# Batch 0's loads dealt anew among three DMA queues, four casts moved to ScalarE, and a block's first sums queued two groups sooner

## The chip, the cores and the metric

One core of one Trainium2 chip. The metric is the device time of one execution in microseconds, median of several executions. A core has five engines: TensorE (PE), VectorE (DVE), ScalarE (ACT), GpSimd (POOL) and SyncE (SP), each of which has its own list of instructions. In the traces here what stands behind a waiting instruction waits too: in the kernel before, VectorE's squares stand 6.60 us behind a transpose whose input has not landed. DMAs are issued from SyncE's, ScalarE's or GpSimd's queue, in that engine's order.

## The reference

Eight batches of 3008 rows. Attention without softmax, gated by u, then a two-layer network:

```python
scores = (z @ z.T) / S                        # z: 3008 x 64
attn   = np.maximum(scores, 0.0) ** 2
x      = u * (attn @ v)                       # u, v: 3008 x 256
h      = x @ w_in                             # 256 -> 2048
g      = h * (1 / (1 + np.exp(-1.702 * h)))
out    = g @ w_out                            # 2048 -> 256
```

## The kernel before

TensorE makes scores (`sc`) in blocks of 256 by 512; ScalarE applies the ReLU (`rl`), VectorE squares (`a`). The scores are symmetric, so half of the blocks are not computed twice: SyncE turns a square block `a` into `tt` by a DMA transpose. The six chunks of 512 rows then gather attention times V in `o`, VectorE multiplies by the turned u (`ut`) into `xt`, and the network follows. The second matmul of the network uses seven products in place of eight, which needs sums of blocks of `g` (S1 to S4, tile `s`), made by VectorE.

The start of batch 0, cut to the parts that change:

```python
def first_cast(g):                            # z to f16, twice, for the first transposes
    m = g % CB * CB
    for c in range(2):
        dve.tensor_copy(ZT["st"][g // CB][:, m:m + CB, c, :], ZT["f"][g // CB][:, m:m + CB, :])

def load_v(b, n0):                            # 4 blocks of V
    ...
    by_pool = b == 0 and n0 < 3 * VB
    dst, eng = V16[b][:, n0:n0 + VB], pool    # GpSimd's DMA casts f32 to f16 on the way
    if by_pool:                               # or: plain f32 load, and GpSimd itself casts
        dst, eng = pa.tile([P, VB, D], F32, ...), act if n0 < 2 * VB else sp
    ...

def load_u(b, i):                             # chunk i of u: 4 DMAs of 128 KB
    uq = pu.tile([P, CH // QW, QW, NCC], F32, name="uq", tag="uq")
    ...
        pool.dma_start(uq[...], src[:, :, cs])

def turn_unit(b, i, jp, a):                   # the transposes, all in SyncE's queue
    ...
    sp.dma_start_transpose(TT[b, i, cj][...], a...)
```

A chunk's steps are numbered, and tables say at which step a load or a turn of u is programmed: an entry `(i, n): k` means chunk i, step n, item k. Loads are programmed on GpSimd; the table `LOADW` holds the loads of W1 and W2. In chunks 2 and 3 of batch 0, step 23 holds a marker on GpSimd that waits for TensorE; what GpSimd has programmed behind it waits too:

```python
def post(last):
    sig = pool.nop()
    for m in last:
        tc.add_manual_dep(sig.ins, m.ins.name, SYNC, reason="row tiles of one bank")
    return sig
...
TURN0 = {(i, (38, 28)[i] if i < 2 else NJ + 4 if i < NCH - 1 else 12): i for i in range(NCH)}
LOAD0 = {(1, 14): 2, (2, 12): 3, (2, NJ + 20): 4, (4, 8): 5}                  # loads of u
LOADW = {(3, 12): 0, (3, 20): 1, (3, 28): 2, (3, 36): 3, (4, 16): 4, ...}     # loads of W1, W2
```

Of the kernel before, what the change touches and what calls it, by code (L numbers as in the profile page):

```python
# [15 lines left out]
def kernel(  # L16
# [13 lines left out]
    AF = mybir.ActivationFunctionType  # L30
# [6 lines left out]
    NJ = (S + P - 1) // P  # L37
# [4 lines left out]
    CB = CH // P  # L42
# [4 lines left out]
    NFG = NFF // FFG  # L47
    QW = 32
# [7 lines left out]
    dve, act, pe, sp, pool = nc.vector, nc.scalar, nc.tensor, nc.sync, nc.gpsimd  # L56
# [21 lines left out]
    ZT, V16, UQ, UT, XT, unit, TT = {}, {}, {}, {}, {}, {}, {}  # L78
# [37 lines left out]
            for h in range(2):  # L116
                eng.dma_start(zf[h * SREM:(h + 1) * SREM, m1 + CB - 1, :], z[0, S0:S])

    def first_cast(g):
        m = g % CB * CB  # L120
        for c in range(2):
            dve.tensor_copy(ZT["st"][g // CB][:, m:m + CB, c, :], ZT["f"][g // CB][:, m:m + CB, :])

    def first_zt(g):

# [33 lines left out]
    VB = 4  # L159
# [3 lines left out]
    def load_v(b, n0):  # L163

        if n0 == 0:
            V16[b] = pz.tile([P, NJ, D], F16, name="V16", tag="V16")
        by_pool = b == 0 and n0 < 3 * VB
        dst, eng = V16[b][:, n0:n0 + VB], pool
        if by_pool:
            dst, eng = pa.tile([P, VB, D], F32, name="vst", tag="tt", bufs=14), act if n0 < 2 * VB else sp  # L170
        full = min(VB, NJ - 1 - n0)
        eng.dma_start(dst[:, :full, :], v[b, n0 * P:(n0 + full) * P].rearrange("(n p) c -> p n c", p=P))
        if full < VB:
            for h in range(2):
                eng.dma_start(dst[h * SREM:(h + 1) * SREM, full, :], v[b, S0:S])
        if by_pool:
            for n in range(0, VB, 2):
                pool.tensor_copy(V16[b][:, n0 + n:n0 + n + 2], dst[:, n:n + 2])

    def width(i):  # L180
        return CH if i < NCH - 1 else LAST

    def load_u(b, i):
        n = width(i)
        uq = pu.tile([P, CH // QW, QW, NCC], F32, name="uq", tag="uq")
        src = u[b, i * CH:i * CH + n].rearrange("(q t) c -> t q c", t=QW)
        for k in range(P // QW):
            cs = slice(k * NCC * QW, (k + 1) * NCC * QW)
            pool.dma_start(uq[k * QW:(k + 1) * QW, :n // QW].rearrange("t q c k -> t q (c k)"), src[:, :, cs])  # L189
        UQ[b, i] = uq  # L190

    def turn_u(b, i):
# [96 lines left out]
    def full(b):  # L289

        return NCH - 2 if b < B - 1 else NCH - 1
# [65 lines left out]
    def blocks(b):  # L357

        return [(i, CH if i < NCH - 1 or b % 2 else LFULL) for i in range(NCH)]

    def up_group(b, q):
        k, fg = divmod(q, NFG)
        i, n = blocks(b)[k]
        hg = ps2.tile([P, FFG, CH], F32, name="hg", tag="ps2")
        for e in range(FFG):
            ff = fg * FFG + e
            for c in range(NCC):
                pe.matmul(  # L368
                    hg[:, e, :n], W1[:, c, ff * P:(ff + 1) * P], XT[b, i][:, c, :n],
                    start=(c == 0), stop=(c == NCC - 1),  # L370
                )
        if fg % 2 == 0:
            GT[b, k, fg // 2] = pa.tile([P, CB, CH], F16, name="gt", tag="tt", bufs=14)
        g = GT[b, k, fg // 2][:, (fg % 2) * FFG:(fg % 2 + 1) * FFG, :n]
        gf = pw.tile([P, FFG, CH], F32, name="gf", tag="gf")
        act.activation(gf[:, :, :n], hg[:, :, :n], AF.Gelu_apprx_sigmoid, scale=1.0 / FSC)  # L376
        if q >= LAGY and q % 4 == 1:
            act.activation(g, gf[:, :, :n], AF.Copy, scale=FSC)  # L378
        else:
            dve.tensor_scalar(g, gf[:, :, :n], FSC, None, ALU.mult)  # L380
        for s_ in [SUMS.pop(0) for _ in range(min(len(SUMS), 1 + (len(SUMS) > 8)))]:
            s_()
        if k < nst(b) and fg == NFG - 1:
            SUMS.extend(left_sums(b, k))



# [4 lines left out]
    def nst(b):  # L392
        return NCH - 1 + b % 2

    SUMS, ST = [], {}
# [26 lines left out]
        g = GT[b, k, h].rearrange("p f (m o t) -> p f m o t", o=2, t=P)  # L422
        return g[:, :, :, odd, :]

    def left_sums(b, k):
        out_ = []
        for name in ("S1", "S2", "S3", "S4"):
            for h in range(2):
                out_.append(lambda name=name, h=h: left_sum(b, k, name, h))
        return out_  # L430

    def left_sum(b, k, name, h):
        a11, a12, a21, a22 = left(b, k, h, 0), left(b, k, h + 2, 0), left(b, k, h, 1), left(b, k, h + 2, 1)
        if name == "S3":
            ST[b, k, name, h] = a21
            dve.tensor_tensor(a21, a11, a21, ALU.subtract)
            return
        s_ = ST[b, k, name, h] = pa.tile([P, CB, 2, P], F16, name="s", tag="a", bufs=26)
        if name == "S1":
            dve.tensor_tensor(s_, a21, a22, ALU.add)  # L440
        elif name == "S2":
            dve.tensor_tensor(s_, ST[b, k, "S1", h], a11, ALU.subtract)  # L442
        else:
            dve.tensor_tensor(s_, a12, ST[b, k, "S2", h], ALU.subtract)  # L444
# [117 lines left out]
    TURN0 = {(i, (38, 28)[i] if i < 2 else NJ + 4 if i < NCH - 1 else 12): i for i in range(NCH)}  # L562
    LOAD0 = {(1, 14): 2, (2, 12): 3, (2, NJ + 20): 4, (4, 8): 5}
    TURN = {(1, NJ + 4): 2, (2, NJ + 4): 3, (4, NJ + 4): 4, (5, 8): 5}
    LOADW = {(3, 12): 0, (3, 20): 1, (3, 28): 2, (3, 36): 3, (4, 16): 4, (4, 22): 5, (4, 28): 6, (4, 34): 7}
    LOAD = {(3, NJ + 20): 4, (4, NJ + 5): 5}

    FIRST_ZT, FIRST_CAST = {16: 4, 25: 5}, {7: 4, 17: 5}
# [23 lines left out]
        load_v(0, n0)  # L592
    first_z(2 * CB, 4 * CB, sp)
    first_z(4 * CB, NJ, sp)
    load_v(0, 3 * VB)
    load_v(0, 2 * VB)
    for n0 in (4 * VB, 5 * VB):
        load_v(0, n0)
    warm_up(7)
    for g in range(2):  # L600
# [9 lines left out]
        post_()  # L610
    turns[0]()
    take(0, 1)
    for i in range(2):
        load_u(0, i)

    for b in range(B):
        nup = NCH * NFG
        more = b + 1 < B
        sched = SCHED0 if b == 0 else SCHED if more else SCHED_LAST
        turn, load = (TURN, LOAD) if b else (TURN0, LOAD0)  # L620
        head = 0
        for i in range(NCH):
            host = b + 1 if more and i == NCH - 1 else b
            if host > b:
                fill(host)
                LATE.append(host)
            for n, step in enumerate(attend(b, i, b == 0 and i < 2)):
                if b == 0 and i == 0 and n == 3:
                    turns[1]()
                if b == 0 and i == 0 and n in FIRST_CAST:  # L630
                    first_cast(FIRST_CAST[n])
                if b == 0 and i == 0 and n in FIRST_ZT:
                    first_zt(FIRST_ZT[n])()
                if (i, n) in turn:
                    turn_u(b, turn[i, n])
                if (i, n) in load:
                    load_u(b, load[i, n])
                if b == 0 and (i, n) in LOADW:
                    load_w(LOADW[i, n])
                if more and (i, n) == (NCH - 2, 2):  # L640
                    load_z(b + 1)
                if (b, i, n) == (0, NCH - 1, NJ + 4):
                    for sum_ in weight_sums():
                        sum_()
                take(host, sched[i].get(n, 0))
                if i == full(b) and n >= HEAD and (n - HEAD) * LAGY // (2 * NJ - 10) >= head and head < LAGY:
                    up_group(b, head)
                    head += 1
                step()
        late.sort(key=lambda t: t[0])  # L650
        if more:
            for i in range(2):
                load_u(b + 1, i)
            for n0 in range(0, NJ, VB):
                load_v(b + 1, n0)
        prods = products(nst(b))
        for q in range(head, nup):
            if more and q in (head + 14, head + 20):
                k = int(q == head + 20)
                turn_u(b + 1, k)  # L660
                load_u(b + 1, k + 2)
            up_group(b, q)
            product(b, *prods.pop(0))
            if q >= 30 and q % 2 and late:
                late.pop(0)[1]()
        steps = [lambda kp=kp: product(b, *kp) for kp in prods]
        if nst(b) < NCH:
            k = NCH - 1
            steps += [lambda s=s: down(b, k, s) for s in range(blocks(b)[k][1] // P)]
        for step in steps:  # L670
            step()
            for sum_ in [SUMS.pop(0) for _ in range(min(len(SUMS), 1 + (len(SUMS) > 4)))]:
                sum_()
            for _, turn_it in [late.pop(0) for _ in range(min(len(late), 1 + (len(steps) < 10)))]:
                turn_it()
        LATE.clear()
        if more:
            while late:
                late.pop(0)[1]()
            take(b + 1, 2)  # L680
# [30 lines left out]
```

## Time and profile before

| | kernel before |
|---|---|
| time, median of 3 executions | 1209.84 us (1204.06 to 1211.1) |
| span of the profiled execution | 1206.6 us |
| TensorE busy / idle | 1187.5 / 19.1 us |
| wait at u of chunk 0 (hole 1) | 4.46 us at 31.09 |
| wait at the 10th transpose (hole 2) | 4.78 us at 51.65 |
| granted clock in 30 to 40 and 50 to 60 us | 0.83 |
| waits for the sums `s`, start to start | 0.67 + 0.37 us, after four of the eight batches |

How to read it: a hole is a stretch in which TensorE, the busiest engine, stands idle. The lines behind the table stand in the prediction below. In them a timeline line reads: start, duration, engine, source line, operation, output and inputs, how many instructions are merged, and in brackets the idle time before and who ended it. The prediction explains the columns of a window line; numbers in parentheses there count instructions.

### The profile page before, as it was taken

How to read it: one execution, taken by the hardware profiler on the slowest of the kernel's cores; microseconds unless marked ns; L12 is line 12 of the kernel's file. 1: busy time of each engine (PE TensorE's matmuls, PEld its weight loads, DVE VectorE, ACT ScalarE, POOL GpSimd, SP SyncE). 2: the span in 40 equal slices, each digit the busy share in tenths (PEclk: the TensorE clock that was granted, in tenths of full speed). 3: DMA queues.
4: the chain of work that ended last, by engine and by line, in shares of the span. 5: the costliest groups of instructions: out<-in, count | busy, mean ns of one | idle time of the engine just before them, and what ended most of it. 6: DMA issues, size and time to landing. Idle time of an engine off the chain costs nothing.

```text
span 1206.6 us, 27543 instructions
## 1 busy us (share of the span) xinstructions
PE 1187.5 (98%) x11427; PEld 722.9 (60%) x11427; DVE 819.4 (68%) x1319; ACT 828.9 (69%) x983; POOL 228.4 (19%) x328
## 2 busy tenths in 40 slices
PE   7899999999999999999999999999999999999998
PEld 2245775457754677546765467654775547855576
DVE  5579756577666785577775777557776477664776
ACT  6587866678666786568865688647876478672785
POOL 4144010331003310023101231013300142001000
PEclk9899999999999999999999999999999999999999
DMA  9999469765698657876567767794578955695012
GB/s 162 158 132 133 97 146 169 92 97 118 118 165 94 94 133 135 135 87 110 132 132 141 77 106 149 145 129 76 94 149 145 125 85 104 146 159 98 1 36 71
DMA packets 371102, 141.02 MB, mean 117 GB/s; under 512 B 313376, under 2 KB 364320, under 8 KB 370976
## 3 DMA queue, kind: packets, MB, share of 16 engines
q1 hardware_dynamic: 310528, 94.67, 43.8%
q0 software_dynamic: 59088, 43.34, 24.3%
q8 instruction: 89, 1.46, 0.5%
q10 hardware_dynamic: 1360, 1.25, 0.3%
q14 instruction: 37, 0.30, 0.1%
HBM read 60.29 MB, written 24.64 MB: 70 GB/s over the span
## 4 chain that ended last, share of the span: by engine, by line
PE 92%; DVE 3%; DMA 2%; ACT 2%; issue 1%; POOL 1%; ACTq 0%; DVEq 0%
PE o L327 38%; PE hg L368 26%; PE st L469 20%; PE sc L227 6%; PE yp L525 2%; ACT gf L376 1%; DMA uq<-in_u_dram 1%; DMA vst<-in_v_dram 1%; DMA tt<-a 1%; DVE gt L380 0%; DVE s L444 0%; DVE s L442 0%; DVE s L440 0%; ACT rl L241 0%; DVE y L485 0%
## 5 line engine op out<-in xcount | busy, mean ns | idle before, releaser
L376 ACT ACTIVATE gf<-hg 128x1024 f32<-128x1024 f32 (+1 forms) x384 | 385.6, 1004 | 137.5 <-PE hg L368 114.6
L241 ACT ACTIVATE rl<-sc 128x1024 f16<-128x1024 f32 x309 | 303.4, 1027 | 163.6 <-PE sc L227 155.7
L327 PEld LDWEIGHTS <-V 64*128 64x128 f16 (+1 forms) x4052 | 239.9, 95 | 242.4 <-issue 15.7
L368 PE MATMUL hg<-xt,W 128*128 128x512 f16 (+1 forms) x1408 | 354.6, 374 | 0.0
L380 DVE TENSOR_SCALAR gt<-gf 128x1024 f16<-128x1024 f32 (+1 forms) x320 | 223.0, 697 | 144.9 <-ACT gf L376 141.5
L327 PE MATMUL o<-a,V 64*128 64x512 f16 (+3 forms) x2286 | 305.3, 370 | 0.2 <-DVE a L255 0.2
L255 DVE TENSOR_TENSOR a<-rl 128x1024 f16<-128x1024 f16 x274 | 189.0, 695 | 163.0 <-ACT rl L241 162.9
L189 POOL DMA_DIRECT2D uq<-in_u_dram x192 | 129.7, 683 | 627.5 <-PE sc L227 372.5
L327 PE MATMUL o<-tt,V 64*128 64x512 f16 (+1 forms) x1510 | 234.9, 377 | 4.8 <-DMA tt<-a 4.8
L368 PEld LDWEIGHTS <-W 128*128 128x128 f16 x1536 | 139.3, 98 | 119.3 <-issue 2.6
L469 PEld LDWEIGHTS <-gt 128*128 128x128 f16 x2816 | 169.5, 98 | 31.9
L469 PEld LDWEIGHTS <-s 128*128 128x128 f16 x2112 | 127.8, 98 | 29.6 <-DVE s L442 4.2
L227 PE MATMUL sc<-ZT 64*128 64x512 f16 (+1 forms) x688 | 122.1, 368 | 5.5 <-ACT rl L241 4.5
L469 PE MATMUL st<-WT,s 128*128 128x128 f16 x1408 | 93.1, 219 | 2.9 <-DVE s L442 2.8
L469 PE MATMUL st<-WT,gt 128*128 128x128 f16 x1408 | 93.0, 219 | 0.0
L469 PE MATMUL st<-W,gt 128*128 128x128 f16 x1408 | 92.3, 219 | 0.0
L479 ACT ACTIVATE uP<-st 128x256 f32<-128x256 f32 x132 | 49.7, 376 | 27.7 <-PE st L469 15.5
L227 PEld LDWEIGHTS <-ZT 64*128 64x128 f16 x688 | 39.0, 94 | 49.3 <-issue 14.4
L485 DVE SCALAR_TENSOR_TENSOR y<-st,uP 128x256 f32<-128x256 f32 x132 | 54.5, 418 | 20.4 <-ACT uP L479 11.4
L378 ACT ACTIVATE gt<-gf 128x1024 f16<-128x1024 f32 (+1 forms) x64 | 66.0, 1031 | 2.0
L344 DVE TENSOR_TENSOR xt<-o,ut 128x512 f16<-128x512 f32 x80 | 51.3, 683 | 22.7 <-PE o L327 22.7
L196 DVE STREAM_TRANSPOSE ut<-uq 128x1024 f32<-128x1024 f32 (+1 forms) x48 | 58.2, 1213 | 6.6 <-DMA uq<-in_u_dram 6.6
(50 smaller groups left out, 613.3 us busy)
## 6 DMA issues: line engine op xcount, KB each, us to landing
uq<-in_u_dram POOLq DMA_DIRECT2D x160, 128.0 KB, 3.6
out_dram<-y SPq DMA_DIRECT2D x40, 512.0 KB, 3.5
V<-in_v_dram POOLq DMA_DIRECT2D x37, 256.0 KB, 6.3
tt<-a SPq DMA_TRANSPOSE x232, 3.7
uq<-in_u_dram POOLq DMA_DIRECT2D x32, 112.0 KB, 4.9
V<-in_v_dram POOLq DMA_DIRECT2D x8, 192.0 KB, 8.0
out_dram<-y POOLq DMA_DIRECT2D x4, 384.0 KB, 3.2
zst<-in_z_dram POOLq DMA_DIRECT2D x7, 192.0 KB, 8.5
```

The lines of the kernel that those rows point to most:

```text
L189: pool.dma_start(uq[k * QW:(k + 1) * QW, :n // QW].rearrange("t q c k -> t q (c k)"), src[:, :, cs])
L196: dve.transpose(ut[:, :, :n // QW, :].rearrange("p k q t -> p q k t"), UQ.pop((b, i))[:, :n // QW].rearrange("p q c k -> p q k c"),)
L227: pe.matmul(sc[:, r, :m * P], zt[h, 2 * kp + r, :], zt[h, (qi + 1) * CB - m:(qi + 1) * CB, :], start=True, stop=True,)
L241: act.activation(rl, sc, AF.Relu, scale=csc)
L255: dve.tensor_tensor(a, rl, rl, ALU.mult)
L327: ins = pe.matmul(acc[c][:, :n], V16[b][h, j].rearrange("p (c k) -> p k c", k=NCC)[:, c], weights(b, i, j)[h], start=(k, m) == first[c], s ...
L368: pe.matmul(hg[:, e, :n], W1[:, c, ff * P:(ff + 1) * P], XT[b, i][:, c, :n], start=(c == 0), stop=(c == NCC - 1),)
L376: act.activation(gf[:, :, :n], hg[:, :, :n], AF.Gelu_apprx_sigmoid, scale=1.0 / FSC)
L378: act.activation(g, gf[:, :, :n], AF.Copy, scale=FSC)
L380: dve.tensor_scalar(g, gf[:, :, :n], FSC, None, ALU.mult)
L469: pe.matmul(bank[:, m, :], lhs()[:, f, m, :], right[:, ff, :], start=name in ("P1", "P2", "P5") and m == 0 and ff == 0, stop=ff == NFF // ...
L485: dve.scalar_tensor_tensor(y[:, :, o, c], ST[b, k, "bank" + x], 1.0 / FSC, ST[b, k, "after" + u_], ALU.mult, ALU.add,)
```

## The change

Its intent: let u of chunk 0 land earlier, by giving it to SyncE and clearing GpSimd's queue of V; relieve VectorE at the start; and give VectorE two fewer sums to do at the end of a batch. The core of the diff:

```diff
     def load_v(b, n0):
-        by_pool = b == 0 and n0 < 3 * VB
         dst, eng = V16[b][:, n0:n0 + VB], pool
-        if by_pool:
+        if b == 0:                                   # all six loads of V as f32, cast by GpSimd
             dst, eng = pa.tile([P, VB, D], F32, ...), act if n0 < 2 * VB else sp
 ...
     def load_u(b, i):
+        eng = pool if b or i else sp                 # u of chunk 0 from SyncE
 ...
-        if k < nst(b) and fg == NFG - 1:
-            SUMS.extend(left_sums(b, k))
+        if k < nst(b) and fg in (NFG - 3, NFG - 1):  # S1, S2 of half 0 two groups sooner
+            SUMS.extend(left_sums(b, k, fg == NFG - 1))
 ...
-    LOADW = {(3, 12): 0, (3, 20): 1, (3, 28): 2, (3, 36): 3, (4, 16): 4, ...}
+    LOADW = {(3, 16): 0, (3, 24): 1, (3, 32): 2, (3, 40): 3, (4, 16): 4, ...}
 ...
-    for i in range(2):
-        load_u(0, i)
+    load_u(0, 1)
 ...
+                if b == 0 and i == 0 and n == 5:
+                    load_u(0, 0)
 ...
-                    first_cast(FIRST_CAST[n])
+                    first_cast(FIRST_CAST[n], True)  # z groups 4 and 5 cast by ScalarE
```

More of the change, by code (lines that the diff above doesn't have):

```diff
@@ L117, in first_z, with first_cast @@
                 eng.dma_start(zf[h * SREM:(h + 1) * SREM, m1 + CB - 1, :], z[0, S0:S])
-    def first_cast(g):
+    def first_cast(g, by_act=False):
         m = g % CB * CB
         for c in range(2):
-            dve.tensor_copy(ZT["st"][g // CB][:, m:m + CB, c, :], ZT["f"][g // CB][:, m:m + CB, :])
+            dst, src = ZT["st"][g // CB][:, m:m + CB, c, :], ZT["f"][g // CB][:, m:m + CB, :]
+            if by_act:
+                act.activation(dst, src, AF.Copy, scale=1.0)
+            else:
+                dve.tensor_copy(dst, src)
     def first_zt(g):
@@ L175, in load_v @@
                 eng.dma_start(dst[h * SREM:(h + 1) * SREM, full, :], v[b, S0:S])
-        if by_pool:
+        if b == 0:
             for n in range(0, VB, 2):
@@ L188, in load_u @@
             cs = slice(k * NCC * QW, (k + 1) * NCC * QW)
-            pool.dma_start(uq[k * QW:(k + 1) * QW, :n // QW].rearrange("t q c k -> t q (c k)"), src[:, :, cs])
+            eng.dma_start(uq[k * QW:(k + 1) * QW, :n // QW].rearrange("t q c k -> t q (c k)"), src[:, :, cs])
         UQ[b, i] = uq
@@ L423, in left, with left_sums @@
         return g[:, :, :, odd, :]
-    def left_sums(b, k):
-        out_ = []
-        for name in ("S1", "S2", "S3", "S4"):
-            for h in range(2):
-                out_.append(lambda name=name, h=h: left_sum(b, k, name, h))
-        return out_
+    def left_sums(b, k, last):
+        some = [("S1", 0), ("S2", 0)]
+        if last:
+            some = [("S1", 1), ("S2", 1)] + [(name, h) for name in ("S3", "S4") for h in range(2)]
+        return [lambda m=m: left_sum(b, k, *m) for m in some]
     def left_sum(b, k, name, h):
@@ L564 @@
     TURN = {(1, NJ + 4): 2, (2, NJ + 4): 3, (4, NJ + 4): 4, (5, 8): 5}
-    LOADW = {(3, 12): 0, (3, 20): 1, (3, 28): 2, (3, 36): 3, (4, 16): 4, (4, 22): 5, (4, 28): 6, (4, 34): 7}
+    LOADW = {(3, 16): 0, (3, 24): 1, (3, 32): 2, (3, 40): 3, (4, 16): 4, (4, 22): 5, (4, 28): 6, (4, 34): 7}
     LOAD = {(3, NJ + 20): 4, (4, NJ + 5): 5}
@@ L594 @@
     first_z(4 * CB, NJ, sp)
-    load_v(0, 3 * VB)
-    load_v(0, 2 * VB)
-    for n0 in (4 * VB, 5 * VB):
+    for n0 in range(2 * VB, NJ, VB):
         load_v(0, n0)
```

## The prediction

> **What bounds the kernel now.** I read the page first, for the busy shares and the chain that ended last:
>
> ```profile
> PE 1187.5 (98%) x11427; PEld 722.9 (60%) x11427; DVE 819.4 (68%) x1319; ACT 828.9 (69%) x983; POOL 228.4 (19%) x328
> PE 92%; DVE 3%; DMA 2%; ACT 2%; issue 1%; POOL 1%; ACTq 0%; DVEq 0%
> ```
>
> TensorE is busy 98% of 1206.6 us, and the same matmuls in the same order are in both programs (the order of the changed kernel shows no difference on TensorE but line numbers). So the change can only win from the 1206.6 - 1187.5 = 19.1 us in which TensorE idles, and from time in which its clock is low. The next question is where those 19.1 us lie. Busy time by stretch says: nearly all before 60 us.
>
> ```profile
> 0.00:10.00 10.00, 7.39 (x39) 2.89 (x40) 5.49 (x13) 6.05 (x8) 3.69 (x11) 1.00 0.76 236
> 20.00:30.00 10.00, 6.63 (x34) 2.05 (x32) 3.18 (x5) 3.74 (x4) 2.04 (x4) 1.00 1.24 105
> 30.00:40.00 10.00, 8.91 (x38) 2.86 (x38) 7.06 (x12) 7.26 (x8) 2.21 (x4) 0.83 1.03 115
> 40.00:50.00 10.00, 6.87 (x44) 2.35 (x42) 6.89 (x10) 6.41 (x7) 2.57 (x4) 1.00 1.23 174
> 50.00:60.00 10.00, 8.32 (x60) 3.53 (x62) 1.98 (x3) 3.59 (x4) 0.00 (x0) 0.83 1.16 181
> 60.00:80.00 20.00, 20.00 (x171) 10.08 (x168) 16.48 (x26) 19.36 (x21) 6.65 (x11) 1.00 1.19 164
> ```
>
> The columns after the stretch are its length, then busy us of TensorE, weight loads, VectorE, ScalarE and GpSimd, the granted clock, the DMA share, GB/s. From 60 to 80 us TensorE never idles; before that it does in two holes, and the clock falls to 0.83 in the window after each. The timeline names both holes, and the waits say who ended them:
>
> ```profile
> 28.10 1.25 DVE L196 STREAM_TRANSPOSE ut<-uq 128x1024 f32<-128x1024 f32 x1 [6.60 <-DMA uq<-in_u_dram]
> 31.09 0.39 PE L227 MATMUL sc<-ZT 64*128 64x512 f16 x2 [4.46 <-ACT rl L241]
> 51.65 0.89 PE L327 MATMUL o<-tt,V 64*128 64x512 f16 x6 [4.78 <-DMA tt<-a]
> ...
> 317.65 0.40 PE L469 MATMUL st<-WT,s 128*128 128x128 f16 x4 [0.51 <-DVE s L442]
> 318.25 1.74 PE L469 MATMUL st<-WT,s 128*128 128x128 f16 x28 [0.20 <-DVE s L442]
> ```
>
> Hole 1: VectorE stands 6.60 us at the transpose of u of chunk 0, because that u has not landed; behind it in order stand the squares, ScalarE runs out of buffers, TensorE out of scores: 4.46 us. Hole 2: TensorE waits 4.78 us for a transposed attention block (tt) that the DMA has not landed. The third kind comes at the end of each odd batch (near 317, 611, 905 and 1197 us): 0.7 to 1.0 us for the sums s. The chain of waits gives the two transfers:
>
> ```profile
> 16.23 11.85 DMA uq<-in_u_dram
> 45.47 6.13 DMA tt<-a
> ```
>
> **What the Trainium skill says.** (1) "TensorE: Matmul & The Clock Gate", Part 1: an idle window of about 3.4 us puts the array at half its clock, and about 3.4 us of work brings it back. The trace agrees: 0.83 over 10 us is (1 - 0.83) x 10 / 0.5 = 3.4 us at half clock after each hole, so each costs another 1.7 us. (2) "DMA: Bandwidth & Descriptors", Queues, rings and completion order: each DMA engine goes round-robin between the queues that have work, packet by packet. The trace agrees: a transpose issued at 17.04 us, with u in flight on GpSimd's queue, took 19.7 us to land; those of 58 to 60 us, with none, 3.4 us. (3) Same page, SWDGE vs HWDGE vs iDMA: a DMA that casts must be GpSimd's. The trace agrees: V in f16 is loaded by POOLq, V in f32 by ACTq or SPq, with 6 casts of 638 ns (median) on GpSimd. (4) "GPSIMD Engine Reference", Key points: GpSimd shares SBUF access with VectorE. A square costs 693 ns (median) but one beside GpSimd's casts and descriptors took 1983 ns.
>
> **The change part by part.**
>
> V of batch 0. Three loads leave GpSimd's queue (256, 256, 192 KB of f16, issued at 9.5 to 14.2 us, landing about 5 to 7 us later) and become f32 loads on SyncE plus 6 more casts. DMA share is 0.53 at 8 to 10 us and 0.04 at 10 to 12 us, so SyncE can put this V (1.4 MB; at the 340 GB/s or so of the first 8 us, some 4.2 us) into a hole of the DMA: estimate, all of V landed near 13.5 us. GpSimd loses 5 issues, about 3.7 us, and gains 6 x 0.62 = 3.7 us of casts: it is free at about 15 us, as before. V block 12 is read at 16 us at the earliest: no new wait.
>
> u of chunk 0. It leaves GpSimd's queue (issued 14.15 to 16.88, last landing 28.08) for SyncE, behind two transposes (the second issued at 12.13), each u DMA also waiting for the DMA whose semaphore it reuses, here the V loads. So issue is at about 13.5 to 16 us. DMA work from there, in time alone: one transpose 1.4 us (the ten that land from 50.75 to 63.04 us come that far apart), a chunk of u about 4.3 us (128 packets of 4 KB at 518 ns each in the packet records, over 16 engines, is 4.1 us, and a start), first u of chunk 0, then u of chunk 1 in competition: landing at 22 to 25 us instead of 28.08. VectorE comes to it at 21.5 us, TensorE has about 2 us of slack: hole 1 shrinks to 0 to 1.5 us, from 4.46. With the low clock gone, 5 to 6.5 us of gain at this point.
>
> Hole 2 then decides. TensorE reaches it some 6 us earlier, at about 40.5 us instead of 46.9. What it waits for is the 10th transpose of SyncE's queue, which is in order: eight blocks, six of them wanted only 15 us and more later, stand ahead, and now also u of chunk 0. DMA work that must be done by then: from about 24 us eight transposes 8 x 1.4 = 11.2 us, u of chunks 2 and 3 at 4.3 each (both are now issued earlier, because the u buffers come free earlier, and go ahead). That is 15.5 to 19.8 us; in the kernel before 10 transposes (14), three V (1536 packets at 64 ns over 16 engines: 6) and four u (17), 37 us, took from 10 to 51.6 us, that is, 0.9 of the time. So the 10th lands at 24 + 17 to 22 = 41 to 46 us: 44.5 as a middle. TensorE waits 1 to 5 us there, and it goes on 51.6 - 44.5 = 7 us earlier than before. If the wait stays under 3.4 us the clock also stays up, another 1.7 us. Estimate for both holes together: 7 us, between 4 and 11.
>
> z casts on ScalarE. Four casts leave VectorE (2 x 0.28 and 2 x 0.36 us) and become four of about 0.35 us on ScalarE, an estimate from its 128x256 ACTIVATE of 376 ns. The first pair fits into ScalarE's gap of 0.70 us before 13.11; the second pushes two ReLUs by about 0.4 us in a loop that ScalarE and TensorE take turns in. Cost: 0.4 us.
>
> W1 loads four steps later: 4 x 0.25 = 1 us, against a first use at 77.2 us and a landing at 70.5: hidden.
>
> Sums. Two of a block's eight sums are queued two groups earlier. At the end of an odd batch VectorE has then two fewer (2 x 0.68 us) to do before the product that waits. By the timeline, the sum that now ends at 318.19 would end near 317.1, while TensorE wants its first half at 316.97 (already done) and its second at 317.4. The wait goes: 0.67 + 0.37 us of start-to-start delay at 317.65 and 318.25, 1.04 us, times 4 batches = 4.2 us; I count 3.8. The amount of VectorE work is the same.
>
> Sum: 7 - 0.4 + 3.8 = 10.4 us. 1209.84 - 10.4 = 1199.4; as the profiled run (1208.38) and the fastest (1204.06) lie under the median, I say 1198.5.
>
> **The rivals.** A: hole 2 takes all that hole 1 gives. For: DMA share is 1.03 to 1.24 from 20 to 60 us, the queue is in order, and u is now ahead of the blocks in the same queue. Against: the V loads move into a stretch where the DMA was idle, so the backlog itself is 4 to 6 us shorter. It would leave only the sums, and a shift of 2 us or so: 1203. B: both holes close (the DMA was slow between 20 and 32 us only because two queues fought, 92 GB/s against 181 before): 4.46 + 4.78 + 2 x 1.7 = 12.6, with small delays about 13, plus 3.8: 1192. C: a new wait in the first 25 us, if six more casts of GpSimd beside VectorE's squares, or ScalarE's casts, slow the loop there: ScalarE is busy 8.32 of 10 us from 10 to 20. One to 2 us lost: 1200. D: TensorE, earlier by 7 to 10 us, runs into W1 or the next batch's z, which have 6 to 7 us of slack now. Against: their issue follows TensorE and moves with it. It would give back 1 to 3 us.
>
> **Range and chances.** A and B bound it: 1203 and 1192, with 1 us for the scatter of the runs: 1191 to 1204 holds it 8 times in 10. 2% is 24 us; all idle time and low clock together are 19.1 + 3.4 us, and 4 us of it is start-up, so faster by over 2% has a chance of 0.01; slower by over 2% would need a new wait of 24 us: 0.01. Within 2%: 0.98.
>
> **What would show it.** In the changed profile: the idle time before the first STREAM_TRANSPOSE falls from 6.60 us to under 2.5; u of chunk 0 lands at 22 to 25 us; the clock in 30 to 40 us is 1.00; TensorE still waits on DMA tt<-a, 1 to 5 us, ending at 41 to 46 us; no wait of TensorE for the sums s near 317, 611, 905, 1197 minus the shift; VectorE's and ScalarE's busy time differ by 1.4 us or less. Wrong if u from SyncE lands after 27 us, if the wait for tt ends after 49 us, or if the waits for s remain.

## More of the kernel before

All timed executions that are compared here were of the fast state. Still, one kernel's executions spread over 2 to 12 us, and the study is partly about what that spread is made of.

## The result and the profile after

The changed kernel took 1194.1 us (median of 4, 1192.45 to 1197.61), the kernel before 1208.89 us (median of 4, 1204.06 to 1211.1): ratio 0.9887, 95% interval 0.9847 to 0.9927. Ratios here are the mean time of one kernel's executions over that of the other's of the same rounds, so not quite the ratio of the medians quoted.

The page of the changed kernel: busy times, and the shares of the chain that ended last.

```profile
PE 1183.7 (99%) x11427; PEld 722.6 (61%) x11427; DVE 820.6 (69%) x1315; ACT 830.5 (70%) x987; POOL 231.9 (19%) x325
PE 98%; ACT 0%; DMA 0%; DVE 0%; issue 0%; SPq 0%; ACTq 0%
```

The span is 1190.8 us, so TensorE idles for 7.1 us in place of 19.1. DMA and VectorE have gone from the chain: what is left is TensorE.

The same stretches as in the prediction:

```profile
0.00:10.00 10.00, 7.21 (x34) 2.48 (x35) 5.23 (x13) 5.33 (x6) 3.46 (x11) 0.89 0.84 272
10.00:20.00 10.00, 9.53 (x51) 3.38 (x51) 5.94 (x9) 9.19 (x14) 9.16 (x12) 0.94 1.16 250
20.00:30.00 10.00, 10.00 (x53) 3.37 (x50) 7.29 (x12) 7.75 (x8) 2.57 (x4) 1.00 1.23 168
30.00:40.00 10.00, 10.00 (x55) 3.56 (x54) 7.42 (x11) 7.90 (x9) 2.57 (x4) 1.00 1.16 190
40.00:50.00 10.00, 9.96 (x95) 4.64 (x91) 6.50 (x10) 7.94 (x9) 0.00 (x0) 1.00 1.18 185
```

Both holes are closed: TensorE is busy without a break from 20 us on, at full clock, and the DMA moves 168 and 190 GB/s where it moved 105 and 115. A low clock shows at another place, 0.89 and 0.94 before 20 us: ((1 - 0.89) + (1 - 0.94)) x 10 / 0.5 = 3.4 us at half speed, which cost 1.7 us. It comes and goes between executions of the same kernel: two of its four profiled executions have it, so it isn't put down to the change.

The timeline where the holes and the waits for the sums were, VectorE at its transpose of u, TensorE at the first use of the 10th transpose and at the sums after batch 1:

```profile
22.71 1.24 DVE L200 STREAM_TRANSPOSE ut<-uq 128x1024 f32<-128x1024 f32 x1
...
41.59 1.03 PE L331 MATMUL o<-tt,V 64*128 64x512 f16 x8
...
304.54 1.06 PE L473 MATMUL st<-W,s 128*128 128x128 f16 x16
305.44 0.78 PE L473 MATMUL st<-WT,s 128*128 128x128 f16 x11
```

None of the four has a bracket, that is, no idle time before it. The last fences are the DMA issues of 14.0 to 16.7 us before, and of 14.4 to 16.6 us after: queue, count, size of each, median time in flight.

```profile
uq<-in_u_dram POOLq DMA_DIRECT2D x4, 128.0 KB, 11.7
tt<-a SPq DMA_TRANSPOSE x2, 13.2
```

```profile
uq<-in_u_dram SPq DMA_DIRECT2D x4, 128.0 KB, 3.5
```

The same u of chunk 0, issued at the same time, is 3.5 us in flight in place of 11.7. Its last part lands at 19.98 us, from the trace's record of that DMA, in place of 28.08.

The gain of the two profiled spans is 1206.6 - 1190.8 = 15.8 us. The known pieces: holes 4.46 + 4.78, the half clock after each 2 x 1.7, the sums 3.9 (measured below), minus 1.7 for the half clock at the start: 14.8. The other 1.0 us is not accounted for.

### The profile page after: what moved, and what is told of

The parts are those of the page before. It is cut to its first block, busy times and chain, and to the rows that moved or that the text cites.

```text
span 1190.8 us, 27541 instructions
## 1 busy us (share of the span) xinstructions
PE 1183.7 (99%) x11427; PEld 722.6 (61%) x11427; DVE 820.6 (69%) x1315; ACT 830.5 (70%) x987; POOL 231.9 (19%) x325
## 3 DMA queue, kind: packets, MB, share of 16 engines
q8 instruction: 89, 1.46, 0.5%
## 4 chain that ended last, share of the span: by engine, by line
PE 98%; ACT 0%; DMA 0%; DVE 0%; issue 0%; SPq 0%; ACTq 0%
PE o L331 40%; PE hg L372 27%; PE st L473 23%; PE sc L231 6%; PE yp L529 2%; DMA zf<-in_z_dram 0%; ACT rl L245 0%; DVE zst L126 0%; DVE a L259 0%; ACT ZT L141 0%; ACT zst L124 0%; DVE y L489 0%; SPq L109 0%; PE zp L133 0%; ACTq L245 0%
## 5 line engine op out<-in xcount | busy, mean ns | idle before, releaser
L483 ACT ACTIVATE uP<-st 128x256 f32<-128x256 f32 x132 | 49.7, 377 | 23.2 <-PE st L473 11.2
L446 DVE TENSOR_TENSOR s<-s,gt 128x1024 f16<-128x1024 f16 x88 | 60.3, 685 | 1.0
```

What stands on the lines that cost most here:

```text
L446: dve.tensor_tensor(s_, ST[b, k, "S1", h], a11, ALU.subtract)
```

## The experiments

Each call ran its kernels on one chip beside the kernel before; the three calls were on three chips. "Issued" and "landed" are from the trace's DMA records.

### The changed kernel again, and its start taken apart (first call)

Kernel before: 1210.31 us, median of 11 (1203.8 to 1212.31). The first kernel is the changed one, unedited.

> The changed kernel again, as the yardstick of this call. The two profiles say: no hole of TensorE after 20 us, u of chunk 0 landed near 20 us, the 10th transpose landed near 37 us. If that is the change and not luck, the same shows here, and the time is 0.986 to 0.992 of the kernel before (14 us less). If the clock was luck (the half-speed window of 3.4 us that the changed kernel had from 7.9 to 11.3 us), its place differs and the time moves by under 2 us.

Measured: 1197.77 us (1191.4 to 1200.8, 6 executions), ratio 0.9901 [0.9871, 0.9931]. It was not the same as the first time, and its profile (span 1196.2) shows hole 2 again. Its timeline, and the chain of waits:

```profile
45.55 1.46 PE L331 MATMUL o<-tt,V 64*128 64x512 f16 x6 [5.21 <-DMA tt<-a]
```

```profile
35.97 9.54 DMA tt<-a
```

The same transpose that took 3.8 us in the first profile (issued 33.45, landed 37.23) took 9.54 us here. What differs is the order of two queues. GpSimd's issue of u of chunk 3, first in the profile without the hole, then in this one:

```profile
36.42 2.57 POOL L193 DMA_DIRECT2D uq<-in_u_dram  x4 [9.60 <-DVE ut L200]
```

```profile
34.79 2.58 POOL L193 DMA_DIRECT2D uq<-in_u_dram  x4 [9.60 <-DVE ut L200]
```

In the first, u3 is issued 3 us behind the transpose's 33.45; in the second 1.2 us ahead of its 35.97, and the last part of u3 and the transpose land together, at 45.47 and 45.51. This became the theory: two queues race, and the changed kernel has a quick and a slow form.

Next, u of chunk 0 put back into GpSimd's queue, V and all else as changed:

```diff
-        eng = pool if b or i else sp
+        eng = pool
...
-    load_u(0, 1)
+    for i in range(2):
+        load_u(0, i)
...
-                if b == 0 and i == 0 and n == 5:
-                    load_u(0, 0)
```

> The changed kernel, but u of chunk 0 goes back to GpSimd's queue, before u of chunk 1. Theory A (the queue of u matters: two chunks of u one behind the other in GpSimd's queue, in turn with the transposes of SyncE's, slow each other down): u of chunk 0 lands at 26 us or later, VectorE waits over 2.5 us at its first transpose, the hole of TensorE comes back with 2 us or more, and the 10th transpose lands after 42 us; 3 to 9 us lost. Theory B (the V loads that cast were what clogged GpSimd's queue; they are still gone here): u of chunk 0, issued near 16.6 us, lands by 24 us, VectorE waits under 1.5 us, and under 1.5 us are lost.

Measured: 1198.08 us (1195.99 to 1200.1), ratio 0.9914 [0.9886, 0.9942]. In the timeline hole 1 is back, smaller:

```profile
26.49 1.25 DVE L200 STREAM_TRANSPOSE ut<-uq 128x1024 f32<-128x1024 f32 x1 [4.87 <-DMA uq<-in_u_dram]
...
29.47 0.39 PE L231 MATMUL sc<-ZT 64*128 64x512 f16 x2 [2.75 <-ACT rl L245]
```

And V as before, with u of chunk 0 left with SyncE:

```diff
+        by_pool = b == 0 and n0 < 3 * VB
...
-        if b == 0:
+        if by_pool:
...
-    for n0 in range(2 * VB, NJ, VB):
+    load_v(0, 3 * VB)
+    load_v(0, 2 * VB)
+    for n0 in (4 * VB, 5 * VB):
```

> The changed kernel, but V is loaded as in the kernel before (three blocks cast by GpSimd's DMA), while u of chunk 0 stays with SyncE. Theory A: u of chunk 0 still lands by 22 us, no hole at the first transpose of u, and under 3 us are lost in all. Theory B: V, in GpSimd's queue until 20 us or so, holds up SyncE's u as it held up GpSimd's: u lands after 24 us, a hole of 1.5 us or more, and the 10th transpose after 42 us; 4 us or more lost. If both losses are small, either part alone would have done.

Measured: 1198.07 us (1194.71 to 1199.17), ratio 0.9909 [0.988, 0.9938]. Hole 1 again, and a wait that is new, at W1:

```profile
26.79 1.25 DVE L201 STREAM_TRANSPOSE ut<-uq 128x1024 f32<-128x1024 f32 x1 [3.91 <-DMA uq<-in_u_dram]
...
29.78 0.39 PE L232 MATMUL sc<-ZT 64*128 64x512 f16 x2 [1.80 <-ACT rl L246]
...
72.87 1.53 PE L373 MATMUL hg<-xt,W 128*128 128x512 f16 x4 [1.95 <-DMA W<-in_moe_w_in_dram]
```

What follows from the two: each half alone leaves VectorE waiting 4 to 5 us for u of chunk 0, and TensorE 1.8 to 2.75 us; only both together close the hole. In both, TensorE came so late to the 10th transpose that it didn't wait for it, though that landed at 44.66 us without the move of u and at 40.35 without the move of V (theory B had said after 42). The 44.66 is a transpose of 9.1 us in flight with u of chunk 2 beside it and u of chunk 3 behind it, so it isn't only u3 that slows one down. Without the move of V, SyncE issued u0 at 13.09 to 16.31 us, but V's casting loads and u1 (from 15.33 us) were in flight from GpSimd's queue, and u0 was up to 11.8 us on the way, landing at 26.67. Without the move of u, GpSimd first did its six more casts, and u0 was issued at 17.30 in place of 14.15, landing at 26.36. The medians of the three kernels don't separate them, because the first one ran mostly in its slow form; the profiles do.

Last, the changed kernel with the old order of the sums (the hunk of `left_sums` undone):

> The changed kernel, but with the sums queued as before. My count says: the four waits of TensorE for the sums at the ends of odd batches come back, 0.67 + 0.37 us of delay each, 4.2 us in all, and nothing else: about 1.0035 of the changed kernel. The rival: those delays were made up elsewhere, and the time is that of the changed kernel within 1 us.

Measured: 1197.82 us (1195.59 to 1202.73), ratio 0.9919 [0.9889, 0.995]. The four waits for `s` are back in the profile, but the time can't be told from the changed kernel's 1197.77 beside it, whose own executions spread over 9.4 us. As a time this run is inconclusive; it was repeated below on a steadier base. Its profile also has a wait of 1.46 us at W1.

### The race taken out (second call)

Kernel before: 1211.71 us, median of 11. First the changed kernel once more:

> The changed kernel a third time, beside the next three. Its runs so far lie between 1191.4 and 1200.8, and of its two profiles one had no hole (1190.8 us) and one had a hole of 5.2 us at the 10th transpose (1196.2 us), with u of chunk 3 issued 1.2 us before that transpose and landed just before it. If the order of these two issues decides it, a profile with u of chunk 3 issued after the 10th transpose has no hole, and one with it before has a hole of 3 us or more. Runs near 1192 and near 1198 are both expected.

Measured: 1192.73 us (1192.66 to 1195.63, 4 executions), ratio 0.9853 [0.9824, 0.9883]: the quick form, no hole. The 10th transpose was issued at 33.88 and landed at 37.58; u3 was issued at 36.49, behind it.

Then a kernel in which u of chunk 3 is programmed behind chunk 2's marker, so that it can't be issued early, and W1's second load ahead of chunk 3's:

```diff
-    LOAD0 = {(1, 14): 2, (2, 12): 3, (2, NJ + 20): 4, (4, 8): 5}
+    LOAD0 = {(1, 14): 2, (2, 26): 3, (2, NJ + 20): 4, (4, 8): 5}
-    LOADW = {(3, 16): 0, (3, 24): 1, ...}
+    LOADW = {(3, 16): 0, (3, 20): 1, ...}
```

> The changed kernel with two moves on GpSimd: u of chunk 3 is loaded behind the marker that waits for step 23 of chunk 2 (position 26 in place of 12), so after the 10th transpose has been used; and the second W1 load stands before the marker of chunk 3 (position 20 in place of 24), so that it is issued right behind the first. If the two transfers are what makes the changed kernel's time scatter, no hole is left between 20 us and 80 us: the profile is at 1189 to 1193 us, and the runs lie within 4 us of each other, 1190 to 1194, 0.983 to 0.987 of the kernel before. Rival: the scatter has other sources (clock, the chip's DMA speed): the runs still lie 6 us or more apart, though the profile shows no such hole.

Measured: 1192.58 us (1191.33 to 1195.5), ratio 0.985 [0.9822, 0.9877], no hole; u3 is issued at 45.17 us. This is the gated kernel of what follows. Its executions lie 4.2 us apart, just over the 4 expected, for one at 1195.5, whose granted clock is 1.000: that one has no half clock behind a hole, and what made it slow is not known. Since the changed kernel ran in its quick form on this chip, the pair shows no difference: the gate costs nothing that can be measured, but this call doesn't show that it helps.

On this base, the old order of the sums:

> The same two moves, but with the sums queued as before. With the scatter gone the sums should be measurable as a time: four waits of 1.04 us come back near 307, 601, 895 and 1188 us, so 4.2 us more than the run with the moves alone. Rival: under 2 us more.

Measured: 1196.45 us (1195.76 to 1198.23), ratio 0.9881 [0.9855, 0.9907]; the timeline at the end of batch 1:

```profile
304.88 0.40 PE L473 MATMUL st<-WT,s 128*128 128x128 f16 x4 [0.51 <-DVE s L446]
305.48 1.74 PE L473 MATMUL st<-WT,s 128*128 128x128 f16 x28 [0.20 <-DVE s L446]
```

The same two lines stand at 598.8, 892.7 and 1184.4 us. 1196.45 - 1192.58 = 3.9 us is what the sums' new order is worth (3.8 by the ratios): nothing else differs, neither profile has a hole, and all five executions of the gated kernel lie under the fastest of these six.

And the last z casts back on VectorE:

```diff
-                    first_cast(FIRST_CAST[n], True)
+                    first_cast(FIRST_CAST[n])
```

> The same two moves, but the last two z casts stay with VectorE. My prediction charged ScalarE's casts with 0.4 us: if so, chunk 1 starts (first read of a transposed block) 0.4 us earlier than in the run with the moves alone, and the time is the same within 1 us. If they cost the 1.3 us by which chunk 1 starts later in the changed kernel's first profile (25.7 against 24.4 us), it starts at 24.4. Rival: VectorE, held up by GpSimd's casts, is late with the z casts and chunk 1 starts later, by 0.5 us or more: then the move to ScalarE is needed because of V's casts.

Measured: 1192.95 us (1192.08 to 1195.73), ratio 0.9853 [0.9823, 0.9883], 0.4 us from the gated kernel, which is within the spread. TensorE waits at the place of the cast:

```profile
14.55 0.40 PE L133 MATMUL zp<-ident,zst 128*128 128x128 f16 x4 [1.24 <-DVE zst L126]
```

and chunk 1 begins (first `o<-tt`) at 24.95 us in place of 24.41 in the gated kernel. So the casts on ScalarE didn't cost the 0.4 us that was predicted; by these two profiles they saved about 0.5 us. That is little more than how much this start varies with the casts on ScalarE: 24.05 to 24.50 us in seven profiles without low clock, and 25.44 in an eighth. Nothing shows in the total.

### Does the order of the two issues make the hole? (third call)

Kernel before: 1210.62 us, median of 11 (1205.49 to 1216.87). The changed kernel and the gated kernel side by side, five rounds each:

> The changed kernel again, beside the three that follow. Its runs so far lie at 1191 to 1194 us where the last load of u chunk 3 is issued behind the 10th transpose of batch 0, and near 1198 us where it is issued ahead of it. Theory R (two queues race): the profiled execution shows either no wait of TensorE at the 10th transpose and a span near 1191 us, or a wait of 4 to 5.5 us near 45 us and a span near 1196 us; in the second case the first load of u3 is issued before the 10th transpose. Rival (the scatter is the chip's clock alone): the order of these two issues does not go with the hole.

> The changed kernel with u chunk 3 loaded behind chunk 2's marker and W1's second load ahead of chunk 3's. Theory R: no wait of TensorE at the 10th transpose in the profile and a median of 1191 to 1194 us, whatever the changed kernel beside it does; if that one shows the hole, this one is 3 to 5 us quicker. Rival (clock alone): the two have the same median within 1.5 us even where the changed kernel shows the hole.

Measured: 1194.05 us (1191.62 to 1198.17) and 1192.28 us (1191.36 to 1193.92); ratios 0.9875 [0.9843, 0.9906] and 0.9855 [0.9829, 0.9881]. Both profiles are without hole 2, and the medians are 1.8 us apart. The gated kernel's has two short waits instead, 0.38 us at 70.39 for W1 and 0.79 us at 76.53 for a later transpose. The changed kernel had three of its six executions at 1195 us and above, the gated kernel none; but the intervals overlap, and no slow execution fell to the profiler.

Within the profiles the effect of u3 on a transpose can be read by itself. The DMA issues of three stretches: first the 9th and 10th transpose of the changed kernel (32.27 and 33.62 us), ahead of its u3 (35.20 to 37.77); then the two it issued at 36.52 and 38.16, at the end of u3's issue and behind it; last the 10th transpose of the gated kernel, issued at 36.95 us with u3 not yet issued:

```profile
tt<-a SPq DMA_TRANSPOSE x2, 3.8
```

```profile
tt<-a SPq DMA_TRANSPOSE x2, 8.6
```

```profile
tt<-a SPq DMA_TRANSPOSE x1, 3.3
```

The gated kernel's 10th transpose was issued later than the one in the slow profile (36.95 against 35.97) and landed 5.2 us sooner (40.29 against 45.51). A late issue alone doesn't make the hole: what the slow profile has, and none of the other profiles of the changed and gated kernels, is u3 issued ahead of its 10th transpose. That is one slow profile; the order of the two issues was not forced.

Then an attempt to force the slow order: u of chunk 1 turned sooner, so that its buffer comes free for u3 sooner.

```diff
-    TURN0 = {(i, (38, 28)[i] if i < 2 else ...
+    TURN0 = {(i, (38, 20)[i] if i < 2 else ...
```

> The changed kernel with the turn of u chunk 1 at step 20 of chunk 1 in place of 28: the buffer of u1 comes free some 2 us sooner, and so the loads of u chunk 3 are issued at about 33 us, always ahead of the 10th transpose. Nothing else moves. Theory R: the profile shows the wait for the 10th transpose (tt) back, 3 to 5.5 us near 45 us, u3 issued before that transpose and both landing within a microsecond of each other, and a median 3 to 6 us above the gated kernel, 1196 to 1198 us. Rival (the transposes ahead in SyncE's own queue set the landing, u3 has no part in it): the 10th transpose lands at 37 to 41 us as in the changed kernel's quick runs, and the median is within 1.5 us of the gated kernel's.

Measured: 1197.29 us (1191.55, 1195.75, 1198.82, 1199.17), ratio 0.9887 [0.985, 0.9924], and the profiled execution was the one at 1191.55. In it u3 was issued at 32.99 us as planned, but the transposes, too, had come quicker, and the 10th was out at 31.30, still ahead. GpSimd's timeline, and the DMA issues of 31 to 32 us (the 9th and 10th transpose):

```profile
32.99 2.57 POOL L193 DMA_DIRECT2D uq<-in_u_dram  x4 [7.39 <-DVE ut L200]
```

```profile
tt<-a SPq DMA_TRANSPOSE x2, 3.4
```

So "always ahead" was wrong: the edit moves the odds and not the order. The median is 5.0 us above the gated kernel's, as the race would have it, but the slow executions weren't profiled, and with four of them I count this as support and not as proof.

The last kernel is the one before with the sums' new order alone:

> The kernel before with the sums' new order alone. Theory: the four sum waits (0.67 and 0.37 us, four times) are gone, both holes of the start stay, and the median is 3.5 to 4.2 us below that of the kernel before (ratio 0.9965 to 0.9971). Rival (the waits only hid another limit of the steady state, which takes their place): less than 1.5 us is gained and other idle time of TensorE appears in the stretches where the waits stood.

Measured: 1207.0 us (1204.48 to 1211.01), ratio 0.9978 [0.995, 1.0007]: 3.6 us below the kernel before by the medians, 2.7 by the ratio, and the interval just includes no gain. No wait for `s` is left in its profile, and no other idle time in the stretches where they stood, so the rival has nothing for it. Both holes stay, and the clock's part in them can be seen in the timeline and two windows, the second from the end of hole 1:

```profile
31.64 0.61 PE L227 MATMUL sc<-ZT 64*128 64x512 f16 x2 [4.75 <-ACT rl L241]
53.32 1.46 PE L327 MATMUL o<-tt,V 64*128 64x512 f16 x6 [4.76 <-DMA tt<-a]
```

```profile
30.00:40.00 10.00, 8.36 (x29) 2.47 (x29) 6.15 (x11) 6.00 (x7) 2.57 (x4) 0.66 1.16 102
31.64:41.64 10.00, 10.00 (x38) 2.96 (x38) 5.93 (x11) 6.13 (x7) 1.12 (x2) 0.71 1.14 115
```

With holes of nearly the same length as in the kernel before, the clock was low for (1 - 0.66) x 10 / 0.5 = 6.8 us here, twice what the profile before shows. Only what lies behind the hole costs time: (1 - 0.71) x 10 = 2.9 us. At hole 2 it is again 6.8 us, and the 10 us behind it, at 0.77, cost 2.3. In the profile before it was 1.7 us each. So a hole's cost in clock differs between executions, and a kernel with holes also scatters more: the granted clock is 0.991 to 0.998 in the executions of the kernel before, and 0.007 of 1210 us is 8.5 us.

### All executions of two kernels together

The 20 timed executions of the changed kernel fall into two groups: ten from 1191.4 to 1192.9 us, ten from 1195.2 to 1200.8, and nothing between. The gated kernel has eleven: ten from 1191.3 to 1194.2 and one at 1195.5. If the gate had no effect, a split of at least this kind (one or none of eleven above 1195, ten of twenty) would have a chance of 2.6%, by the counts alone; the border was drawn after seeing the times, and the chips differ. The granted clock is 0.9993 in the mean of the quick ten and 0.9975 in the slow ten, that is, 0.0018 x 1195 = 2.2 us of the 5.0 us between the groups' means. So the slow executions ran longer at half clock, as behind a hole, but the clock alone doesn't make the groups: 2.8 us are left, which waits of TensorE like that of the slow profile can explain. The gated kernel (1192.58 and 1192.28 us) is the best version here, by what it avoids: its quick executions are no quicker than the changed kernel's.

## Why the prediction was right, and where it was not

**The bound and the place of the gain: right.** All but about 1 us of it came from the two holes, the clock behind them and the waits for `s`. All 20 executions, 1191.4 to 1200.8 us, lie in the predicted range of 1191 to 1204; the middle, 1198.5, was 4.4 us above the first median of 1194.1.

**Hole 1, "0 to 1.5 us, from 4.46": right, at its lower end.** The step before it was mis-sized: u was to land at 22 to 25 us because u of chunk 1 was counted as a full competitor. It landed at 19.98; u1 was issued from 16.57 us, when u0 was already out. Part of that was luck: GpSimd was to be free for u1 at about 15 us, with casts of 0.62 us; the eight casts from 9.89 us on took 6.74 us, 0.84 each, and so kept u1 out of u0's way. The idle time before VectorE's transpose is 0, where I had put under 2.5. The two single-part experiments show why: the V loads had to leave GpSimd's queue *and* u0 had to leave it. The prediction had both facts, but gave no account of either alone.

**Hole 2, "TensorE waits 1 to 5 us": this term was mis-sized.** The holes and the clock behind them gave 4.46 + 4.78 + 3.4 = 12.6 us in the quick form, where the prediction had 7; most of the difference is here. The prediction had the 10th transpose land at 41 to 46 us; in five of the six profiles of kernels that keep V, u0 and the place of u3's load as changed, it landed at 34.7 to 38.3 us, with no wait. Two summands were too large. Eight transposes were counted at 1.4 us each, read from landings that SyncE's issue paced, one every 1.35 us or so; in the first profile the 4th to 9th landed in two bunches (4.3 us apart, with u of chunk 2 in flight), within them at gaps of 0.63 to 1.16 us, 0.87 in the mean. And u of chunk 3, 4.3 us, was counted in the middle and upper part of the range as going ahead, while in those five it is issued 1.6 to 3 us behind the 10th transpose. With 0.87 and without u3, and the prediction's own divisor of 0.9: 24 + (8 x 0.87 + 4.3) / 0.9 = 36.5, against 37.23 measured. This sum was fitted after the result and is no test; in that profile only seven of the eight were still to land at 24 us. The prediction also took the clock to stay up behind a wait of less than 3.4 us. No run has so short a wait at this hole, and two waits elsewhere speak against it: behind the 2.75 us without the move of u, and the 1.95 us at W1 without the move of V, the next 10 us have a clock of 0.83. In the sixth profile u3 went ahead, the transpose landed at 45.51 and the wait was 5.2 us, what the prediction had at its upper end. So rivals A and B were not two guesses of which one is true, but near to two forms in which the kernel runs: B's 1192 is the quick group's time, and the slow group, 1195 to 1201, lies between B and A, around the predicted 1198.5.

**The sums, 3.8 us counted (4.2 in full): right.** Measured 3.9 on the gated base; 3.6 by the medians (2.7 by the ratio) alone on the old kernel, with a wide interval.

**The z casts, cost 0.4 us: no cost was found, and it is too small to matter.** By single profiles about 0.5 us of the start is saved, nothing measurable in the total. Rival C, a slower start, did not come: chunk 1 begins at 24.05 us in the slow profile and at 24.41 in the gated kernel's, against 24.40 before; the 25.68 of the first profile has 1.7 us of half clock in it.

**The W1 loads, "four steps later: 1 us, hidden": wrong in size.** GpSimd's timeline before, then after:

```profile
64.23 1.43 POOL L406 DMA_DIRECT2D W<-in_moe_w_in_dram  x2
70.93 1.39 POOL L406 DMA_DIRECT2D W<-in_moe_w_in_dram  x2 [5.26 <-PE sc L227]
```

```profile
52.70 0.72 POOL L410 DMA_DIRECT2D W<-in_moe_w_in_dram  x1
59.40 2.10 POOL L410 DMA_DIRECT2D W<-in_moe_w_in_dram  x3 [5.99 <-PE sc L231]
```

Before, the first two loads go out together and the third waits for TensorE. After, already the second waits: step 24 is behind the marker of step 23, step 20 was ahead of it. It left 6.7 us after the first, where in the gated kernel, with step 20 again, it left 0.7 us after. In the first profile it still landed 3.5 us before its use. In three profiles it did not: 1.95 and 1.46 us of waiting, with the load 11.2 and 10.7 us in flight, and 0.25 us in the changed kernel of the third call. With step 20 the second load was never waited for, but two of the four profiles of gated kernels wait for the first or third, 0.16 and 0.38 us. So rival D was real, in the smaller part of its range or below it, and not in every execution.

**What stays open.** Why a transpose and a load from two queues cost each other more than the sum of what each takes alone is not explained: 92 GB/s in 20 to 32 us before, with a DMA share over 1, and 164 after. And no slow execution but one was profiled; that all ten have hole 2 is inferred from their times and clocks. One gated execution, at 1195.5 us with full clock, must have another cause.

## What to carry to other kernels

In an in-order queue, a load's place relative to a wait on that queue matters more than its distance in steps: four steps were worth 0.7 or 6.7 us. When a kernel's times fall into two groups, compare profiles of both and look for two queues whose order of issue isn't fixed; then fix it by placing the load that isn't urgent behind something that the urgent one precedes. And when one load is late, look at what is in flight beside it before moving it: here moving u alone or V alone left 1.80 or 2.75 of the 4.46 us.

## What the Trainium skill lacked or had wrong

- "DMA: Bandwidth & Descriptors", Queues, rings and completion order: the page has the round-robin between queues, and the runs agree in kind, but it gives no size for what it does to a DMA transpose. Here a 128x1024 f16 transpose was 3.3 to 3.8 us in flight with little or no load beside it, 8.6 to 9.5 us beside u of chunk 3 (512 KB) from GpSimd's queue, and up to 19.7 us in the kernel before.
- Same page: it has a bandwidth for a DMA transpose (not in its section DMA Transpose), but no pace at which transposes of this size can be issued, which set the landings that the prediction read. SyncE issued one every 1.35 us or so, and bunches of them landed 0.63 to 1.16 us apart. The prediction took the first for the second, one of the two reasons why it was too high.
- "TensorE: Matmul & The Clock Gate", Part 1: the clock is halved after at least one idle window of about 3.4 us, and the window runs on its own, whatever the kernel does. The second part fits: in the clock records the half-clock stretches at holes 1 and 2 begin 20.48 us apart both in the kernel before (31.79 and 52.27 us) and with the sums alone (30.67 and 51.15), six times 3.41, and they last 3.41 us in one and 6.83 in the other, though the holes are 4.5 to 4.8 us long in both. The first part is too weak: waits of 2.75 and 1.95 us were followed by 3.41 us at half clock, one of 1.80 us by none. A hole shorter than the window is not safe.
- "GPSIMD Engine Reference": it doesn't spell out that a wait placed on GpSimd for another purpose holds back the loads that it issues behind it; here the second W1 load left 6.7 us after the first in place of 0.7.
